# Linear attention on one core: the first loads as row halves on two queues, two more crossbar blocks of 128 rows, and a shorter warming matmul

## The chip, the core and the metric

The kernel runs on one core of one Trainium2 chip. The core has five engines with an instruction stream each: TensorE (PE; its weight loads are shown apart as PEld), VectorE (DVE), ScalarE (ACT), GpSimd (POOL) and SyncE (SP). SP and ScalarE also issue DMA transfers, each on a hardware queue of its own; in the profile SP's queue is q1 and ScalarE's is q10. The metric is the device time of one execution in microseconds. A profile is one more execution, recorded by the hardware profiler; its span runs from the first to the last recorded instruction.

## The reference

x has 2048 rows of 640 columns, wqkv is 640 x 1920, wo is 640 x 640, all bf16. There are 32 heads of 20 columns.

```python
qkv = (x @ wqkv)                       # split into q, k, v, 32 heads of 20
phi = lambda t: where(t > 0, t + 1, exp(t)) + 1e-6
pq, pk = phi(q), phi(k)
kv  = einsum("bhsd,bhse->bhde", pk, v)
z   = einsum("bhsd->bhd", pk)
num = einsum("bhqd,bhde->bhqe", pq, kv)
den = einsum("bhqd,bhd->bhq", pq, z)[..., None] + 1e-6
return merge_heads(num / den) @ wo
```

## The kernel before

Rows are worked in 16 tiles of 128, columns in five blocks of 128. A small planner (`Plan`) holds one list of operations for each engine, in the order in which they are added, and derives the semaphore waits from the tiles that an operation reads and writes. Each engine runs its list in order, so the order of the code is the order of the work. Each DMA has a semaphore of its own and counts as done when all of its bytes have landed.

The stages are these. First k = x Wk for all 16 tiles (`k_half`, L293): TensorE needs x transposed, xT, with the 640 columns of x on the partitions in five blocks, and the five row blocks of Wk, wk0 to wk4. `k_phi` applies phi on ScalarE and VectorE. Then P = xᵀ pk is accumulated over the tiles (`p_step`, L320), which needs x untransposed (`xn`), in turns with the q tiles (`q_tile`, L346). The state, the denominators and the product with wo follow (L433, L457, L475), and the last stage is the output matmuls (L497).

xT comes in two ways. For the first two row tiles (`NPE = 2`) plain DMAs load x into `xn`, TensorE transposes it against an identity (`transpose_x`, L199), and VectorE and ScalarE copy the results from PSUM to xT (L211; ScalarE takes the first two column blocks of tile 1). For rows 256 to 2047, `load_xT` issues DMA transposes (the crossbar) on SP's queue, L185: four blocks of 128 rows (tiles 2 to 5), then five of 256 (two tiles each). `XCH` lists the row ranges. The first of them waits until x tile 0 has landed.

The head of the two DMA queues, `load_wk`, is written out by hand. A word such as "x01" is x tile 0 (from 0, up to 1) and "w23" is Wk block 2:

```python
for eng, what in (("sp", "x01 w01 w23 w45"), ("act", "x12 w12 w34")):
```

So SP issues x tile 0, wk0, wk2 and wk4, ScalarE x tile 1, wk1 and wk3, each one a transfer of 128 rows of 1280 bytes. Behind its four SP has the crossbar blocks, and then `load_rest`: wqn (the weights of q), x tiles 2 to 15 in three transfers, the weights of v, and wo.

While these land, TensorE runs `warm`, matmuls on a constant whose results nobody reads:

```python
warm(512, 512, 512, 512, 512, 512)
order = "t0 t1 k00 k10 k01 k11 k02 k12 k03 k13 k04 k14"
```

"t0" transposes tile 0, and "k10" multiplies tile 1 with wk0, in two halves of 320 output columns. Tiles 0 and 1 are thus worked together, one Wk block after another: two tiles by two halves are four matmuls for each block. From tile 2 on each tile takes its ten matmuls in one go.

Of the kernel before, what the change touches and what calls it, by code (L numbers as in the profile page):

```python
# [82 lines left out]
def bass_standalone__linear_attn_block__prompt_kernel(nc, x, wqkv, wo, out):  # L83
    B, S, D = x.shape
# [10 lines left out]
    with contextlib.ExitStack() as ctx:  # L95
        es = ctx.enter_context

        def sb(name, cols, dt=BF16):
            return es(nc.sbuf_tensor(name, [128, cols], dt))

        xT = sb("xT", NC_ * S)
        xn = sb("xn", NT * D)
        wk = sb("wk", NC_ * D)
# [29 lines left out]
        P = Plan(nc, es)  # L133

        def bank(b, n=BK, off=0, parts=128):
            return ps[0:parts, BK * b + off:BK * b + off + n]
# [9 lines left out]
        def pool_const():  # L146
# [27 lines left out]


        NPE = 2
        XCH = [(128 * t, 128 * t + 128) for t in range(NPE + 4)] + [
            (a, min(a + 256, S)) for a in range(128 * NPE + 512, S, 256)]

        def xch_of(row):  # L180
            return next(i for i, (a, b) in enumerate(XCH) if a <= row < b)

        def load_xT():
            for i, (a, b) in enumerate(XCH[NPE:]):
                P.add("sp", lambda e, a=a, b=b: e.dma_start_transpose(  # L185
                    xT[:, :].rearrange("p (c s) -> p c s", s=S)[:, :, a:b], x[0, a:b, :]),
                    reads=[("xn", 0)] if i == 0 else [],
                    writes=[("xT", NPE + i)], dma=True)

        def transpose_x(st, b_lo, b_hi):  # L190
            groups = ((0, 2, b_lo), (2, NC_, b_hi))

            def columns(b):
                return bank(b, HALF).bitcast(BF16).rearrange("p (c s) -> p c s", s=128)

            def mm(lo, hi, b):
                def go(e):
                    for c in range(lo, hi):
                        r = e.transpose(columns(b)[:, c, :],  # L199
                                        xn[:, st * D + 128 * c:st * D + 128 * c + 128],  # L200
                                        ident[:, :])
                    return r
                P.add("pe", go, reads=xn_keys(st) + ["ident"], writes=[("bank", b)])
            if b_lo == b_hi:
                mm(0, NC_, b_lo)
            else:
                for g in groups:
                    mm(*g)
            for lo, hi, b in groups:
                eng = "act" if st == 1 and lo == 0 else "dve"  # L210
                P.add(eng, lambda e, lo=lo, hi=hi, b=b, eng=eng: (  # L211
                    e.copy if eng == "act" else e.tensor_copy)(
                    xT[:, :].rearrange("p (c s) -> p c s", s=S)[
                        :, lo:hi, 128 * st:128 * st + 128], columns(b)[:, lo:hi, :]),
                    reads=[("bank", b)], writes=[("xT", st, lo)])

        def xT_keys(a, b, cs=range(NC_)):
            keys = []
            for i, (p, q) in enumerate(XCH):
                if p < b and a < q:  # L220
                    keys += [("xT", i)] if i >= NPE else sorted(
                        {("xT", i, 0 if c < 2 else 2) for c in cs})
            return keys
# [7 lines left out]
        def load_xn(a, b, eng):  # L231
            P.add(eng, lambda e: e.dma_start(
                xn[:, a * D:b * D].rearrange("p (t n) -> p t n", n=D),
                x[0, 128 * a:128 * b, :].rearrange("(t p) n -> p t n", p=128)),
                writes=[("xn", t) for t in range(a, b)], dma=True)

        def load_wk():
            tl = mybir.InstLoadActFuncSet(
                name=nc.get_next_instruction_name(),
                act_func_set_id=ACT_TABLE_SET_LN_EXP, ins=[], outs=[])  # L240
            P.add("act", lambda e: e.add_instruction(tl), writes=["table"])
            for eng, what in (("sp", "x01 w01 w23 w45"), ("act", "x12 w12 w34")):
                for k in what.split():
                    a, b = int(k[1]), int(k[2])
                    if k[0] == "x":
                        load_xn(a, b, eng)
                    else:
                        P.add(eng, lambda e, a=a, b=b: e.dma_start(
                            wk[:, a * D:b * D].rearrange("p (c n) -> p c n", n=D),
                            wqkv[128 * a:128 * b, D:2 * D].rearrange("(c p) n -> p c n", p=128)),  # L250
                            writes=[("wk", c) for c in range(a, b)], dma=True)

        def xn_keys(t):
            return [("xn", t)]

        def load_rest():
            w_cols(wqn, 0, D, 0, "wqn", "sp")
            for a, b in ((2, 6), (6, 11), (11, 16)):
                load_xn(a, b, "sp")
            w_cols(wv, 0, D, 2 * D, "wv", "sp")  # L260
            P.add("sp", lambda e: e.dma_start(
                wog[0:GW, 0:5 * D].rearrange("p (g n) -> p g n", n=D),
                wo[0:5 * GW, :].rearrange("(g p) n -> p g n", p=GW)),
                writes=["wog"], dma=True)
            P.add("sp", lambda e: e.dma_start(
                wog[0:gsz[5], 5 * D:6 * D], wo[5 * GW:D, :]), writes=["wog5"], dma=True)
# [12 lines left out]
        def warm(*cols):  # L279
            for n in cols:  # L280
                P.add("pe", lambda e, n=n: e.matmul(
                    bank(4, n), one[:, 0:128], one[:, 0:n], start=True, stop=True),
                    writes=[("bank", 4)])

        def k_banks(st):
            return (2, 0, 4, 6)[st] if st < 4 else 2 + 2 * ((st - 1) % 3)

        def k_half(st, h, cs=range(NC_)):
            b = k_banks(st)

            def mm(e):
                for c in cs:
                    r = e.matmul(  # L293
                        bank(b + h, HALF),
                        xT[:, c * S + 128 * st:c * S + 128 * st + 128],
                        wk[:, c * D + HALF * h:c * D + HALF * (h + 1)],
                        start=(c == 0), stop=(c == NC_ - 1))
                return r
            P.add("pe", mm, reads=xT_keys(128 * st, 128 * st + 128, cs) + [("wk", c) for c in cs],
                  writes=[("bank", b + h)])  # L300

        def k_phi(st):
# [13 lines left out]
        def p_step(h, st, ds=range(NC_)):  # L316

            def mm(e):
                for d in ds:
                    r = e.matmul(  # L320
                        bank(d, HALF), xn[:, st * D + 128 * d:st * D + 128 * d + 128],
                        pk[:, st * D + HALF * h:st * D + HALF * (h + 1)],
                        start=(st == 0), stop=(st == NT - 1))
                return r
            P.add("pe", mm, reads=xn_keys(st) + [("pk", st)],
                  writes=[("bank", d) for d in ds])
# [223 lines left out]

        pool_const()
        load_wk()
        load_xT()
        load_rest()
        warm(512, 512, 512, 512, 512, 512)
        order = "t0 t1 k00 k10 k01 k11 k02 k12 k03 k13 k04 k14"
        for k in order.split():
            st = int(k[1])
            if k[0] == "t":
                transpose_x(st, *((6, 5), (7, 4))[st])  # L560
            else:
                for h in range(2):
                    k_half(st, h, (int(k[2]),))
        for st in range(2):
            k_phi(st)
        for st in range(2, NT):
            k_half(st, 0)
            k_half(st, 1)
            k_phi(st)
            if st in (4, 5):  # L570
                p_step(0, st - 4, range(2))
            if st >= NT - 2:
                permute_wq((0,) if st == NT - 2 else range(1, NC_))
# [139 lines left out]
```

## Time and profile before

| | us |
|---|---|
| median of three timed runs | 99.47 |
| lowest and highest | 99.46, 100.04 |
| the profiled execution | 99.94 |
| its span | 98.7 |

| engine | busy, us | share of the span |
|---|---|---|
| VectorE | 74.7 | 76% |
| ScalarE | 51.0 | 52% |
| GpSimd | 3.5 | 4% |

How to read the profile's rows. The page groups instructions by line, engine and operation. The chain of work that ended last is followed back from the last instruction, from each step to what released it. A row of it gives its start, its length and the engine, line and count. A timeline row has start, length, engine, line, operation, what is written and read, the form, the count, and in brackets the idle time before it with what ended it. A q behind an engine's name marks its sequencer; for a DMA the length is that of the issuing instruction, and the landing comes later. Busy times of matmuls overlap, because they are pipelined: the pace is read from start to start. A row of a stretch gives from and to, the length, busy time and count by engine, the granted TensorE clock (1 is full speed), the busy share of the 16 DMA engines and GB/s. A row on a queue in a stretch gives packets, megabytes and the share of the 16 engines' time. A row of DMA issues ends with the median time from issue to landing.

### The profile page before, as it was taken

How to read it: one execution, taken by the hardware profiler on the slowest of the kernel's cores; microseconds unless marked ns; L12 is line 12 of the kernel's file. 1: busy time of each engine (PE TensorE's matmuls, PEld its weight loads, DVE VectorE, ACT ScalarE, POOL GpSimd, SP SyncE). 2: the span in 40 equal slices, each digit the busy share in tenths (PEclk: the TensorE clock that was granted, in tenths of full speed). 3: DMA queues.
4: the chain of work that ended last, by engine and by line, in shares of the span. 5: the costliest groups of instructions: out<-in, count | busy, mean ns of one | idle time of the engine just before them, and what ended most of it. 6: DMA issues, size and time to landing. Idle time of an engine off the chain costs nothing.

```text
span 98.7 us, 1679 instructions
## 1 busy us (share of the span) xinstructions
PE 95.4 (97%) x656; PEld 62.5 (63%) x662; DVE 74.7 (76%) x139; ACT 51.0 (52%) x84; POOL 3.5 (4%) x15
## 2 busy tenths in 40 slices
PE   6999999999999999999999999999999999999992
PEld 2567777777777666656676556755446776667771
DVE  0214987888889897999959769999979995929332
ACT  5105553455599202472342476289796749665322
POOL 6800000000000000000000000000000000000000
DMA  1995799979999930000000000006410233321534
GB/s 22 362 214 122 153 173 145 219 209 368 375 362 328 207 77 3 0 0 0 0 7 0 0 0 0 0 0 165 115 62 0 92 107 133 133 73 66 199 133 133
DMA packets 17236, 11.73 MB, mean 119 GB/s; under 512 B 9933, under 2 KB 17229, under 8 KB 17229
## 3 DMA queue, kind: packets, MB, share of 16 engines
q1 hardware_dynamic: 16653, 11.10, 42.3%
q10 hardware_dynamic: 576, 0.53, 1.5%
q8 instruction: 5, 0.08, 0.4%
q14 instruction: 2, 0.02, 0.1%
HBM read 5.90 MB, written 2.62 MB: 86 GB/s over the span
## 4 chain that ended last, share of the span: by engine, by line
PE 87%; DVE 6%; DMA 3%; ACT 1%; issue 1%
PE ps L293 23%; PE ps L497 22%; PE ps L346 21%; PE ps L320 17%; DMA xn<-in_x_dram 3%; DVE za L367 3%; PE ps L457 2%; PE ps L433 1%; DVE pq L361 1%; PE ps L199 1%; ACT eq L354 1%; PE ps L475 1%; DVE eq L358 1%; DVE pt L335 0%; PE ps L407 0%
## 5 line engine op out<-in xcount | busy, mean ns | idle before, releaser
L320 PE MATMUL ps<-pk,xn 128*128 128x320 bf16 x160 | 24.0, 299 | 0.0
L346 PE MATMUL ps<-xT,wqp 128*128 128x512 bf16 x95 | 23.1, 379 | 0.3
L293 PE MATMUL ps<-wk,xT 128*128 128x320 bf16 x160 | 23.0, 305 | 0.0
L497 PE MATMUL ps<-w2p,pq 128*128 128x320 bf16 (+3 forms) x170 | 22.3, 291 | 0.1
L354 ACT ACTIVATE eq<-ps 128x512 bf16<-128x512 f32 x20 | 11.9, 597 | 17.1 <-PE ps L346 17.0
L320 PEld LDWEIGHTS ps<-pk,xn 128*128 128x128 bf16 x160 | 15.6, 98 | 7.5
L293 PEld LDWEIGHTS ps<-wk,xT 128*128 128x128 bf16 x160 | 15.9, 100 | 6.5 <-ACT xT L211 0.2
L497 PEld LDWEIGHTS ps<-w2p,pq 128*128 128x128 bf16 x170 | 15.9, 98 | 6.3 <-DVE pq L489 0.2
L306 ACT ACTIVATE ek<-ps 128x640 bf16<-128x640 f32 x16 | 11.2, 704 | 11.8 <-PE ps L293 11.2
L346 PEld LDWEIGHTS ps<-xT,wqp 128*128 128x128 bf16 x100 | 9.7, 98 | 9.2
L361 DVE SCALAR_TENSOR_TENSOR pq<-ps,eq 128x512 bf16<-128x512 f32 x20 | 13.8, 692 | 0.7
L311 DVE SCALAR_TENSOR_TENSOR pk<-ps,ek 128x640 bf16<-128x640 f32 x16 | 13.2, 824 | 0.5
L422 DVE SCALAR_TENSOR_TENSOR ua<-pq,zc,ua 128x512 f32<-128x512 bf16 x12 | 9.0, 748 | 1.1 <-ACT ua L418 0.9
L308 DVE TENSOR_SCALAR ek<-ek 128x640 bf16<-128x640 bf16 x16 | 5.2, 325 | 6.0 <-ACT ek L306 6.0
L489 DVE TENSOR_TENSOR pq<-pq,rd 128x512 bf16<-128x512 bf16 x20 | 7.4, 418 | 2.8 <-ACT rd L482 2.8
L358 DVE TENSOR_SCALAR eq<-eq 128x512 bf16<-128x512 bf16 x20 | 5.8, 289 | 3.4 <-ACT eq L354 3.2
L534 ACT CAST osb<-ps 128x640 bf16<-128x640 f32 x9 | 6.2, 688 | 3.6 <-PE ps L497 3.4
L522 DVE CAST osb<-ps 128x320 bf16<-128x320 f32 (+2 forms) x8 | 3.5, 435 | 3.3 <-PE ps L497 3.1
L367 DVE TENSOR_TENSOR za<-pk 128x1280 f32<-128x1280 bf16 x4 | 5.8, 1483 | 0.0
L519 ACT CAST osb<-ps 128x320 bf16<-128x320 f32 (+1 forms) x8 | 3.1, 404 | 4.7 <-PE ps L497 4.5
L367 DVE TENSOR_TENSOR za<-za 128x1280 f32<-128x1280 f32 x3 | 4.4, 1483 | 0.0
L271 ACT COPY wqp<-wqn 128x640 bf16<-128x640 bf16 x5 | 4.3, 934 | 0.0
(43 smaller groups left out, 45.2 us busy)
## 6 DMA issues: line engine op xcount, KB each, us to landing
out_dram<-osb SPq DMA_DIRECT2D x15, 160.0 KB, 1.8
xn<-in_x_dram SPq DMA_DIRECT2D x2, 800.0 KB, 10.4
wqn<-in_wqkv_dram SPq DMA_DIRECT2D x1, 800.0 KB, 6.6
wv<-in_wqkv_dram SPq DMA_DIRECT2D x1, 800.0 KB, 13.7
wog<-in_wo_dram SPq DMA_DIRECT2D x1, 750.0 KB, 13.5
w2p<-w2g SPq DMA_DIRECT2D x5, 150.0 KB
xn<-in_x_dram SPq DMA_DIRECT2D x1, 640.0 KB, 7.8
wk<-in_wqkv_dram SPq DMA_DIRECT2D x3, 160.0 KB, 4.1
```

The lines of the kernel that those rows point to most:

```text
L293: r = e.matmul(bank(b + h, HALF), xT[:, c * S + 128 * st:c * S + 128 * st + 128], wk[:, c * D + HALF * h:c * D + HALF * (h + 1)], start=(c ...
L306: P.add("act", lambda e: e.activation(fold(t[:, :]), two_banks(b), ACTF.Exp), reads=banks + ["table"], writes=[("ek", st % 3)])
L311: P.add("dve", lambda e: e.scalar_tensor_tensor(fold(pk[:, st * D:(st + 1) * D]), two_banks(b), 0.0, fold(t[:, :]), ALU.max, ALU.add), rea ...
L320: r = e.matmul(bank(d, HALF), xn[:, st * D + 128 * d:st * D + 128 * d + 128], pk[:, st * D + HALF * h:st * D + HALF * (h + 1)], start=(st ...
L346: r = e.matmul(bank(b), wqp[:, d * D + 128 * c:d * D + 128 * c + 128], xT[:, d * S + BK * sbk:d * S + BK * (sbk + 1)], start=(d == 0), sto ...
L354: P.add("act", lambda e: e.activation(t[:, :], bank(b), ACTF.Exp), reads=[("bank", b), "table"], writes=[("eq", i)])
L358: P.add("dve", lambda e: e.tensor_scalar(t[:, :], t[:, :], 1.0, 1e-6, ALU.min, ALU.add), reads=[("eq", i)], writes=[("eq", i)])
L361: P.add("dve", lambda e: e.scalar_tensor_tensor(pq[:, c * S + BK * sbk:c * S + BK * (sbk + 1)], bank(b), 0.0, t[:, :], ALU.max, ALU.add), ...
L367: P.add("dve", lambda e: e.tensor_tensor(d_ap, a, b, ALU.add), reads=ra + rb, writes=[dst])
L422: P.add("dve", lambda e: e.scalar_tensor_tensor(dst[:, :], v, z, a[:, :], ALU.mult, ALU.add), reads=[("pq", s, c), "zc", key], writes=[dkey])
L489: P.add("dve", lambda e: e.tensor_tensor(v, v, rd[i][:, BK * o:BK * (o + 1)], ALU.mult), reads=[("rd", sbk), ("pq", sbk, c)], writes=[("pq ...
L497: r = e.matmul(bank(b, hi - lo), pq[:, c * S + 128 * st:c * S + 128 * st + 128], w2p[:, c * D + lo:c * D + hi], start=(c == 0), stop=(c == ...
```

## The change

The first four transfers of 128 rows (x tiles 0 and 1, wk0 and wk1) become two of 64 rows each. Rows 0 to 63 of each go on SP's queue, and rows 64 to 127 on ScalarE's, in the same order on both: x tile 0, x tile 1, wk0, wk1. The whole blocks wk2, wk3 and wk4 then all go on ScalarE's queue, which issues seven transfers instead of three; SP issues four, as before, now of 64 rows. Whoever reads one of the four split tiles waits for both of its halves; among them is the first crossbar block on SP's queue.

The crossbar blocks become six of 128 rows (tiles 2 to 7) and four of 256. The last of the six warming matmuls has 128 columns in place of 512. Nothing else differs: the order of the operations on TensorE, VectorE and GpSimd is the same, and so is that on ScalarE behind its loads.

```diff
         NPE = 2
-        XCH = [(128 * t, 128 * t + 128) for t in range(NPE + 4)] + [
-            (a, min(a + 256, S)) for a in range(128 * NPE + 512, S, 256)]
+        SPLIT = (0, 1)
+        XCH = [(128 * t, 128 * t + 128) for t in range(NPE + 6)] + [
+            (a, min(a + 256, S)) for a in range(128 * NPE + 768, S, 256)]
...
-                    reads=[("xn", 0)] if i == 0 else [],
+                    reads=xn_keys(0) if i == 0 else [],
...
-            for eng, what in (("sp", "x01 w01 w23 w45"), ("act", "x12 w12 w34")):
+            for eng, what in (("sp", "h00 h10 g00 g10"), ("act", "h01 h11 g01 g11 w23 w34 w45")):
                 for k in what.split():
                     a, b = int(k[1]), int(k[2])
                     if k[0] == "x":
                         load_xn(a, b, eng)
+                    elif k[0] == "h":
+                        P.add(eng, lambda e, a=a, b=b: e.dma_start(
+                            xn[64 * b:64 * b + 64, a * D:(a + 1) * D],
+                            x[0, 128 * a + 64 * b:128 * a + 64 * b + 64, :]),
+                            writes=[("xn", a, b)], dma=True)
+                    elif k[0] == "g":
+                        P.add(eng, lambda e, a=a, b=b: e.dma_start(
+                            wk[64 * b:64 * b + 64, a * D:(a + 1) * D],
+                            wqkv[128 * a + 64 * b:128 * a + 64 * b + 64, D:2 * D]),
+                            writes=[("wk", a, b)], dma=True)
...
         def xn_keys(t):
-            return [("xn", t)]
+            return [("xn", t, 0), ("xn", t, 1)] if t in SPLIT else [("xn", t)]
...
-            P.add("pe", mm, reads=xT_keys(128 * st, 128 * st + 128, cs) + [("wk", c) for c in cs],
+            P.add("pe", mm, reads=xT_keys(128 * st, 128 * st + 128, cs)
+                  + [("wk", c, b) for c in cs if c < 2 for b in range(2)]
+                  + [("wk", c) for c in cs if c > 1],
...
-        warm(512, 512, 512, 512, 512, 512)
+        warm(512, 512, 512, 512, 512, 128)
```

## The prediction

> **What bounds the kernel now.** I read the page first (engines, then the chain that ended last), then the chain in order of time, then the timeline of the first 13 us, since everything that the diff touches lies there. From the page:
>
> ```profile
> PE 95.4 (97%) x656; PEld 62.5 (63%) x662; DVE 74.7 (76%) x139; ACT 51.0 (52%) x84; POOL 3.5 (4%) x15
> ```
>
> The chain in order of time:
>
> ```profile
> 0.80 2.81 DMA xn<-in_x_dram
> 3.61 0.05 issue
> 3.66 1.25 PE ps L199 x10
> 4.91 7.48 PE ps L293 x50
> ...
> 12.65 1.36 PE ps L293 x10
> ...
> 14.28 13.58 PE ps L293 x100
> 27.87 4.89 PE ps L320 x36
> ```
>
> TensorE is the bound, and the only piece of the chain in the first 28 us that isn't TensorE is the landing of x tile 0 at 0.80 + 2.81 = 3.61 us. From 3.66 on TensorE works without a hole. So the change can act in two ways only: by when TensorE starts on tile 0, and by how fast or how interrupted it runs just after. The timeline of the head:
>
> ```profile
> 0.82 0.39 ACTq L232 DMA_DIRECT2D xn<-in_x_dram  x1
> 0.83 2.72 PE L281 MATMUL ps<-const-bfloat16-1.0 128*128 128x512 bf16 x6 [0.83 <-PEq L698]
> ...
> 1.25 1.37 SPq L248 DMA_DIRECT2D wk<-in_wqkv_dram  x3
> 1.25 0.94 ACTq L248 DMA_DIRECT2D wk<-in_wqkv_dram  x2
> ...
> 3.63 12.05 SPq L185 DMA_TRANSPOSE xT<-in_x_dram  x8
> ...
> 4.62 0.37 ACT L211 COPY xT<-ps 128x256 bf16<-128x256 bf16 x1 [2.55 <-PE ps L199]
> ...
> 4.70 7.68 PE L293 MATMUL ps<-wk,xT 128*128 128x320 bf16 x50
> ```
>
> The warming matmuls end at 0.83 + 2.72 = 3.55, just ahead of the tile. TensorE's pace changes inside the 50 matmuls, which the busy time of L293 alone shows:
>
> ```profile
> 4.69:6.02 1.33, 1.32 (x5) 0.72 (x6) 1.00 1.18 298
> ```
>
> Five 320-column matmuls in 1.33 us are 0.266 us each; the chain above has ten of them in 1.36 us at 12.65, 0.136 each. The granted clock column reads 1.00 here all the same, so the step is to be read from the spacing. If n of the 50 ran at 0.266, n x 0.266 + (50 - n) x 0.136 = 7.48 gives n = 5 to 6: the step to full speed lies near 4.70 + 6 x 0.266 = 6.3 at the latest, about 6.1.
>
> **The halves of x.** Before, tile 0 is alone on SP's queue and tile 1 on ScalarE's; landings follow from issue plus time to landing:
>
> ```profile
> xn<-in_x_dram ACTq DMA_DIRECT2D x1, 160.0 KB, 3.0
> wk<-in_wqkv_dram SPq DMA_DIRECT2D x1, 160.0 KB, 3.2
> wk<-in_wqkv_dram ACTq DMA_DIRECT2D x1, 160.0 KB, 3.4
> wk<-in_wqkv_dram SPq DMA_DIRECT2D x1, 160.0 KB, 4.1
> wk<-in_wqkv_dram ACTq DMA_DIRECT2D x1, 160.0 KB, 4.7
> wk<-in_wqkv_dram SPq DMA_DIRECT2D x1, 160.0 KB, 4.5
> ```
>
> That is x0 3.61, x1 3.82, wk0 4.45, wk1 4.65, then wk2 5.8 (issued at 1.25 + 1.37/3), wk3 6.4 (1.25 + 0.47), wk4 6.7. From x1 to wk1 two tiles take 0.83 us: 0.42 per tile, the engines being full. What the two queues had moved early, from 1.8 to 2.5 and from 2.5 to 3.2 us:
>
> ```profile
> q1 hardware_dynamic: 44, 0.06, 64.3%
> q10 hardware_dynamic: 2, 0.00, 1.6%
> ```
> ```profile
> q10 hardware_dynamic: 114, 0.14, 54.7%
> q1 hardware_dynamic: 105, 0.12, 47.7%
> ```
>
> ScalarE's queue (q10) starts late. At 2.5 us, 44 of x0's 128 row packets are through, and the remaining 84 share the engines one to one with x1's: 168 packets, at 219 in 0.7 us some 0.54 us. After the change a queue holds 64 of x0's rows, then 64 of x1's. If ScalarE's lag stays as it is, x0 is complete when its 64 are, together with 64 of SP's: 128 packets, 0.41 us, a gain of 0.13. If both queues start together, all of x0 goes ahead of all of x1 and it lands one tile before the pair is complete: 3.82 - 0.42 = 3.40, a gain of 0.21. Above that, a pair that starts sooner could give up to 0.4; below, the gain is nothing or a small loss if the second issue on each queue (one costs 0.39 to 0.47) holds something up. I take 0.20, nearer to the row of the full engines: x0 at 3.41, transposes at 3.46.
>
> **Shorter warming.** Six matmuls of 512 columns cost 2.72 us with a tail; starts are about 0.43 apart, so the sixth, begun at 2.9, blocks the array to about 3.35. With 128 columns it blocks to about 3.03. Both lie ahead of 3.41, so the cut itself gives nothing and costs nothing on the path, unless x0 lands before 3.35. It leaves an idle stretch of 3.46 - 3.03 = 0.4 us where before there were 3.66 - 3.35 = 0.3.
>
> **What an earlier start is worth.** 0.20 us of earlier work is added at the low pace. If the step to full speed stays at its place (6.1), half of it is kept, 0.10; if it moves along, all 0.20. I take 0.15.
>
> **The rest of the head.** x1 lands with the pair, at 3.8 or a little before; its transposes come after five of x0's ten (1.25/10 each, less overlap about 0.11), at 3.46 + 0.53 = 3.99: 0.2 to spare. The k matmuls need wk0 at 4.70, wk1 at 4.70 + 4 x 0.266 = 5.76, wk2, wk3 and wk4 at about 6.6, 7.1 and 7.7, all 0.2 sooner now. Seven tiles in the same order at 0.42 each give wk0 at about 4.2, wk1 4.65, wk2 5.1, wk3 5.5, wk4 5.9; ScalarE issues them in steps of 0.47 (0.94 for two), its seventh at 0.82 + 6 x 0.47 = 3.6, so that even a landing 3.0 after issue (the row of x1) is 6.6 for wk4, and 4.7 for a wk0 issued at 1.7. This last is the one narrow place: a bound of 0.2 us of wait against 4.5, from a row with a slow start in it; from the packet rates no wait. ScalarE's queue is issuing until 0.82 + 7 x 0.47 = 4.1; behind it stands the copy that ran at 4.62 and would now run at 4.42. Hidden, 0.3 to spare.
>
> **The crossbar blocks.** Issue and landing of the four blocks of 128 rows, then of the five of 256:
>
> ```profile
> L185 SPq DMA_TRANSPOSE xT<-in_x_dram x4: 1262/1282/1313, 3.6 to 7.6; - x4
> ...
> DMA to landing us min/median/max: 3.0/3.5/3.7
> ```
> ```profile
> L185 SPq DMA_TRANSPOSE xT<-in_x_dram x5: 1400/1898/2212, 8.9 to 15.7; - x5
> ...
> DMA to landing us min/median/max: 4.4/4.7/5.4
> ```
>
> The first waits for both halves of x0 and starts at 3.43 instead of 3.63. Behind this wait on SP stand only the other blocks and the later loads. Tiles 6 and 7 landed at 8.9 + 4.5 = 13.4 against a need at 14.28 and now come as two blocks: tile 6 issued at 3.43 + 4 x 1.33 = 8.75, landed by 12.4; tile 7 by 13.8 against 15.4. The first block of 256 (tiles 8 and 9) issues at about 11.4 and lands at 15.8 to 16.8; the need is 14.28 + 2 x 1.36 - 0.2 = 16.8. Covered, barely at the worst. One long issue (1.4 to 2.2) becomes two of 1.3, so all that follows on SP comes 0.4 to 1.2 later, less 0.2:
>
> ```profile
> wqn<-in_wqkv_dram SPq DMA_DIRECT2D x1, 800.0 KB, 6.6
> ...
> xn<-in_x_dram SPq DMA_DIRECT2D x1, 640.0 KB, 7.8
> ```
> ```profile
> 17.97 0.58 SPq L226 DMA_DIRECT2D wqn<-in_wqkv_dram  x1
> 18.61 2.27 SPq L232 DMA_DIRECT2D xn<-in_x_dram  x3
> ```
> ```profile
> 27.15 0.91 ACT L271 COPY wqp<-wqn 128x640 bf16<-128x640 bf16 x1
> ```
>
> wqn landed at 24.6 for a copy at 27.15, x tile 2 at 26.4 for the products that begin at 27.87 (tile 2 after four matmuls, 28.4). At least 1.0 is left of both. No gain, no cost.
>
> **Sum.** -0.15 (bounds -0.4 and +0.1). The profiled execution took 99.94 us with a span of 98.7, 0.47 above the median 99.47 of the three timed runs (99.46 to 100.04). Its own sum is 99.79; on the median it is 99.32, and I forecast 99.3.
>
> **Rivals.** *The halves bring nothing.* The second half is late on ScalarE's queue by as much as the first is early, x0 lands at 3.6, and only the idle stretch grows: 99.45 to 99.5. For it: the rows of q10. Against it: the packet count above still leaves 0.13. The Trainium skill's "DMA: Bandwidth & Descriptors" (Rules for kernel authors) speaks for it too: two transfers to disjoint partition halves share the same 16 engines, so one should not bother. The rows agree that the engines are shared, but here the halves change which tile goes first, not the rate.
>
> *The step to full speed comes late* (slower). This decides if the step needs TensorE to be busy for some stretch with few holes: the hole ahead of tile 0 grows from 0.3 to 0.4 us (0.6 if x0 isn't early), and activity before it may no longer count. Price: the step came 6.1 - 0.83 = 5.3 us after the first warming matmul; if that count starts again at 3.46 it comes at 8.7, and 2.6 us more at half pace lose 1.3, less the gain of 0.15 to 0.2: 100.6. If the step is only put off by the 0.3 us cut from the warming, 99.5. Against it: the hole of 0.3 was tolerated, and 0.1 more is little. By the Trainium skill's "TensorE: Matmul & The Clock Gate" (Part 1) the pace is set by a free-running window of about 3.4 us; missing one would cost an estimated 1.7 us instead, about 101; no row here shows a window.
>
> *The step comes early.* The runs differ by 0.6 us among themselves, and nothing in the middle can absorb that, so its place may vary. If it fell at the first transposes, (6.1 - 3.66)/2 = 1.2 us and the 0.2 would be gained: 98.1; half of that, 98.7.
>
> *A load comes late*: wk0, wk1 or tile 8 by 0.2 to 0.6, 99.5 to 99.9. For it, ScalarE's queue carries five tiles instead of three; against it, the packet rates.
>
> **Chances.** Forecast (99.0 to 99.45) 0.50; halves without effect 0.14; late step 0.20 (0.16 of it above 1%); early step 0.11, most of it over 1% faster; late load 0.05. A difference of 1% (0.99 us) is about what a measurement of this kernel can tell from no change. Faster by that: 0.11; slower: 0.16; within: 0.73. The range leaves out the full late step and the far end of the early one: 98.7 to 100.4.
>
> **What would show it.** The first transpose at 3.4 to 3.5 and x0's landing at 3.4 (right), or at 3.6 (halves without effect). The spacing of L293 falling from 0.266 to 0.136 at about 6.1: at 8 or later the late step is right. No idle time ahead of L293 between 4.5 and 8.2; if there is, a weight block is late. Tile 8's block landed by 16.6. The forecast is wrong if any TensorE idle stretch shows after the first transpose.

## The result and the profile after

The changed kernel takes 103.97 us (median of six executions, 102.39 to 104.43), the kernel before 99.65 (six, 99.37 to 100.04). The ratio is 1.035, with a 95% interval of 1.030 to 1.040. Ratios here and below count only the executions within 1.5% of the fastest of their kernel, medians count all, so the two can differ where executions lie in two groups. The profiled execution took 103.48 us with a span of 102.2; the span is 3.5 us longer than before. The forecast was 99.3.

The page of the changed kernel, its engines and its chain:

```profile
PE 97.7 (96%) x662; PEld 62.3 (61%) x662; DVE 74.7 (73%) x139; ACT 51.1 (50%) x84; POOL 3.5 (3%) x15
...
PE 90%; DMA 5%; ACTq 2%; ACT 1%; DVE 0%; issue 0%
```

The chain in order of time, which before went from the landing of x0 straight to TensorE (its pieces named issue, 0.03 to 0.05 us between these, are left out here):

```profile
0.81 0.61 ACT L242
1.45 0.86 ACTq L249
2.34 0.62 ACTq L254
2.99 0.62 ACTq L254
3.64 5.07 DMA wk<-in_wqkv_dram
8.75 7.15 PE ps L304 x42
```

Two kinds of piece are new: ScalarE's queue issuing one transfer after another until 3.61 us, and a transfer of a Wk block (wk2) that takes 5.07 us. TensorE enters the chain at 8.75 instead of 3.66. The timeline of the head, with the issues and TensorE's pieces:

```profile
0.80 1.24 SPq L249 DMA_DIRECT2D xn<-in_x_dram  x2
...
0.84 1.47 ACTq L249 DMA_DIRECT2D xn<-in_x_dram  x2
...
2.08 1.24 SPq L254 DMA_DIRECT2D wk<-in_wqkv_dram  x2
...
2.34 1.27 ACTq L254 DMA_DIRECT2D wk<-in_wqkv_dram  x2
...
3.44 9.63 SPq L186 DMA_TRANSPOSE xT<-in_x_dram  x7
3.45 0.69 PE L200 MATMUL ps<-ident,xn 128*128 128x128 bf16 x5 [0.21 <-issue]
...
3.64 1.84 ACTq L259 DMA_DIRECT2D wk<-in_wqkv_dram  x3
...
4.51 0.69 PE L200 MATMUL ps<-ident,xn 128*128 128x128 bf16 x5 [0.37 <-DMA xn<-in_x_dram]
...
5.46 1.23 PE L304 MATMUL ps<-wk,xT 128*128 128x320 bf16 x4 [0.26 <-issue]
...
6.99 1.25 PE L304 MATMUL ps<-wk,xT 128*128 128x320 bf16 x4 [0.30 <-DMA wk<-in_wqkv_dram]
```

The first transpose starts at 3.45. Then TensorE stands still four times: ahead of tile 1 (3.45 + 5 x 0.107 = 3.98, next start 4.51), ahead of wk0 (5.04 to 5.46), wk1 (6.53 to 6.99) and wk2 (8.05 to 8.75). That is 0.53 + 0.42 + 0.46 + 0.70 = 2.1 us. One issue of a half takes about 0.62 us (1.24 for two), where a whole tile took 0.39 to 0.47. The second half of x1 on ScalarE's queue took 0.86, and each of the three whole blocks behind the halves 0.53 to 0.64.

The pace of the k matmuls, the stretch 8.75 to 11.42 and the next:

```profile
8.75:11.42 2.67, 2.67 (x11) 1.34 (x12) 1.00 1.19 211
11.42:12.78 1.36, 1.36 (x12) 0.98 (x11) 1.00 0.99 203
```

(The counts include one or two that overlap the edge.) Ten matmuls fill the 2.67 us at 0.267 us each, and from 11.4 on ten take 1.36. So 18 k matmuls ran at half pace, against five or six before: 12 x 0.131 = 1.6 us. The step to full speed came at 11.4 us instead of 6.1. Together: 2.1 of standing, 1.6 of half pace, 0.21 gained at the start; 3.5, as the spans say. Behind tile 1's last k matmul the distance stays the same: the 100 k matmuls that began at 14.28 begin at 17.80, the last 80 matmuls at 90.70 instead of 87.17.

The landings of the later halves of x1, wk0 and wk1, then of wk2 and wk4:

```profile
xn<-in_x_dram ACTq DMA_DIRECT2D x1, 80.0 KB, 2.9
...
wk<-in_wqkv_dram ACTq DMA_DIRECT2D x1, 80.0 KB, 3.0
...
wk<-in_wqkv_dram ACTq DMA_DIRECT2D x1, 80.0 KB, 4.0
```
```profile
wk<-in_wqkv_dram ACTq DMA_DIRECT2D x1, 160.0 KB, 5.1
```
```profile
wk<-in_wqkv_dram ACTq DMA_DIRECT2D x1, 160.0 KB, 5.8
```

x1's later half is there at 1.45 + 2.9 = 4.4 (3.82 before), wk0's at 2.34 + 3.0 = 5.3 (4.45), wk1's at 2.99 + 4.0 = 7.0 (4.65), wk2 at 3.64 + 5.1 = 8.7 (5.8), wk4 at 4.83 + 5.8 = 10.7 (6.7). The rates beside them. First the kernel before, then the changed one:

```profile
2.80:3.60 0.80, 0.75 (x2) 0.00 (x0) 0.00 (x0) 0.00 (x0) 0.80 (x3) 1.00 1.06 387
3.60:4.40 0.80, 0.74 (x8) 0.75 (x9) 0.29 (x1) 0.00 (x0) 0.66 (x4) 1.00 1.03 359
```
```profile
2.80:3.60 0.80, 0.59 (x4) 0.18 (x3) 0.00 (x0) 0.00 (x0) 0.80 (x3) 1.00 0.89 189
3.60:4.40 0.80, 0.54 (x5) 0.28 (x3) 0.51 (x2) 0.00 (x0) 0.66 (x4) 1.00 0.80 192
4.40:5.20 0.80, 0.69 (x5) 0.45 (x5) 0.14 (x1) 0.00 (x0) 0.23 (x1) 1.00 0.80 250
5.20:6.00 0.80, 0.54 (x3) 0.19 (x4) 0.36 (x1) 0.37 (x1) 0.00 (x0) 1.00 1.20 179
```

The last column, GB/s, is about halved in the first two rows, while the DMA share beside it falls only from 1.03 to 1.06 to 0.80 to 0.89: the engines are mostly not idle, but for the same bytes they are held 1.5 to 1.7 times as long.

### The profile page after: what moved, and what is told of

It is laid out like the page before. It is cut to its first block, busy times and chain, and to the rows that moved or that the text cites. A ratio compares the mean times of both kernels' runs of the same rounds, so it can differ in the third digit from the quotient of the medians.

```text
span 102.2 us, 1694 instructions
## 1 busy us (share of the span) xinstructions
PE 97.7 (96%) x662; PEld 62.3 (61%) x662; DVE 74.7 (73%) x139; ACT 51.1 (50%) x84; POOL 3.5 (3%) x15
## 4 chain that ended last, share of the span: by engine, by line
PE 90%; DMA 5%; ACTq 2%; ACT 1%; DVE 0%; issue 0%
PE ps L304 22%; PE ps L510 21%; PE ps L333 21%; PE ps L359 21%; DMA wk<-in_wqkv_dram 5%; PE ps L470 2%; PE ps L446 1%; ACTq L254 1%; PE ps L488 1%; ACTq L249 1%; ACT L242 1%; PE ps L420 0%; DVE osb L535 0%
## 5 line engine op out<-in xcount | busy, mean ns | idle before, releaser
L304 PE MATMUL ps<-wk,xT 128*128 128x320 bf16 x160 | 24.9, 318 | 1.1 <-DMA wk<-in_wqkv_dram 0.8
L359 PE MATMUL ps<-xT,wqp 128*128 128x512 bf16 x100 | 24.2, 379 | 0.0
L319 ACT ACTIVATE ek<-ps 128x640 bf16<-128x640 f32 x16 | 11.2, 704 | 14.4 <-PE ps L304 13.8
```

Source lines behind the costliest of these rows:

```text
L304: r = e.matmul(bank(b + h, HALF), xT[:, c * S + 128 * st:c * S + 128 * st + 128], wk[:, c * D + HALF * h:c * D + HALF * (h + 1)], start=(c ...
L319: P.add("act", lambda e: e.activation(fold(t[:, :]), two_banks(b), ACTF.Exp), reads=banks + ["table"], writes=[("ek", st % 3)])
L359: r = e.matmul(bank(b), wqp[:, d * D + 128 * c:d * D + 128 * c + 128], xT[:, d * S + BK * sbk:d * S + BK * (sbk + 1)], start=(d == 0), sto ...
```

## The experiments

Three questions: which part of the change does the harm, what makes the halves slow, and what makes the later Wk blocks slower still.

**The two small edits alone.**

```diff
-XCH: four blocks of 128 rows, then 256      warm(512, 512, 512, 512, 512, 512)
+XCH: six blocks of 128 rows, then 256       warm(512, 512, 512, 512, 512, 128)
```

> The kernel before with only the two small edits: six crossbar blocks of 128 rows and the last warming matmul of 128 columns. Theory H (halves): the harm comes from the transfers of 64 rows, whose issue takes 0.6 us against 0.43 for 128 rows, so that the first four tiles arrive at half the rate; then this kernel stays within 0.3 us of before (99.4 to 99.9). Theory Q (queue): the harm comes from wk2 to wk4 standing last on ScalarE's queue and moving beside the crossbar's packets; the same, 99.4 to 99.9. Theory W (warming): the shorter warming puts off the step of TensorE to full speed; 100.2 to 101 and the step in the spacing of the k matmuls at 7 us or later instead of 6.1.

Ratio 1.003 (1.000 to 1.005), median 99.94 against 99.78. TensorE in the head:

```profile
4.73 7.10 PE L293 MATMUL ps<-wk,xT 128*128 128x320 bf16 x50
```

The first 1.36 us of these fifty hold nine, where the kernel before has six in its first 1.36 us: the step came by 4.7 here, ahead of the first k matmul and earlier than in the kernel before. Theory W falls.

**The queue alone**, whole tiles:

```diff
-("sp", "x01 w01 w23 w45"), ("act", "x12 w12 w34")
+("sp", "x01 w01"), ("act", "x12 w12 w23 w34 w45")
```

> The kernel before with whole tiles, but wk2 and wk4 on ScalarE's queue: SP issues x0 and wk0, ScalarE x1, wk1, wk2, wk3, wk4. Theory H: no 64-row transfers, so wk4 is issued by 3.2 us, is there by 6.7, and the time is that of before, 99.4 to 99.9. Theory Q: the weights on the other queue share the engines with the crossbar blocks, wk3 and wk4 land at 7.5 us or later, TensorE waits for them, 100.5 to 102.

Ratio 0.998 (0.996 to 1.001). ScalarE issued its last block at 2.7 and wk4 landed at 6.6, as H said. Moving the blocks is harmless by itself.

**The halves alone**, wk2 and wk4 on SP's queue as before:

```diff
-("sp", "x01 w01 w23 w45"), ("act", "x12 w12 w34")
+("sp", "h00 h10 g00 g10 w23 w45"), ("act", "h01 h11 g01 g11 w34")
```

> x0, x1, wk0 and wk1 as row halves on both queues, but wk2 and wk4 behind them on SP's queue (ahead of the crossbar) and wk3 on ScalarE's; warming and crossbar blocks as before. Theory H: x1 lands at about 4.3, wk0 at 5.3 and wk1 at 6.3 as in the changed kernel, wk2 to wk4 follow within 1.5 us; TensorE waits 1.5 to 2 us and the step to full speed comes late; 101.5 to 103.5. Theory Q: with the weights ahead of the crossbar the waits for wk1 and wk2 go, which are more than half of the loss; 99.8 to 101.

Ratio 1.016 (1.011 to 1.021), median 101.22, just under H's range. x1 landed at 4.7, wk0 at 5.1, wk1 at 7.0 and wk4 at 8.1. So the halves alone cost 1.6%, the queue alone nothing, and both together 3.5%: the rest arises only where the halves make the blocks late and wk2 to wk4 all stand behind them on ScalarE's queue.

**Only x in halves**, Wk whole:

```diff
-("sp", "x01 w01 w23 w45"), ("act", "x12 w12 w34")
+("sp", "h00 h10 w01 w23 w45"), ("act", "h01 h11 w12 w34")
```

> Only x0 and x1 as row halves on both queues; the five blocks of Wk whole and on the queues of before, warming and crossbar blocks as before. Theory H: x0 at 3.4, x1 at 4.3, wk0 at about 5.0, the rest soon after, for two issues more of 0.6 us a queue: a wait of 0.5 us for x1 and 0.4 for wk0, 100.2 to 101.5. Theory Q: nothing is moved behind the crossbar's start, 99.3 to 99.9.

Ratio 1.007 (1.004 to 1.010), from five executions of 100.1 to 100.5, at the lower end of H and above Q. Five more took 101.7 to 102.2, the profiled one among them, so its trace doesn't explain the ratio.

**Which rows, which shape.** Is it that a half reaches only 64 neighbouring partitions? Every second row instead:

```diff
-xn[64 * b:64 * b + 64, ...], x[0, 128 * a + 64 * b:128 * a + 64 * b + 64, :]
+xn[b:128:2, ...],            x[0, 128 * a + b:128 * a + 128:2, :]      (Wk alike)
```

> The changed kernel with one thing different: each half holds every second row (even rows on SP's queue, odd rows on ScalarE's) and so goes to every second partition of all 128, not to the upper or lower 64. The same 64 rows per transfer, the same queues and order. Theory P (partitions): the transfer to 64 neighbouring partitions moves at half rate because it reaches only half of the memory's inlets; then x1 lands by 3.9, wk0 by 4.4, wk1 by 5.0, the DMA engines move over 330 GB/s between 2.8 and 4.8 us, and the time is 99.5 to 100.8. Theory H (issue): a transfer of 64 rows takes 0.6 us to issue whatever the rows are; the landings stay at 4.4, 5.4 and 6.9 and the time at 103 to 104.5.

Median 103.9 (102.08 to 105.03). The rates after 2.8 and 3.6 us stay low, and the halves issue as slowly (0.56 to 0.75 us each):

```profile
2.80:3.60 0.80, 0.60 (x4) 0.16 (x3) 0.00 (x0) 0.00 (x0) 0.80 (x3) 1.00 0.88 202
3.60:4.40 0.80, 0.56 (x5) 0.29 (x3) 0.50 (x2) 0.00 (x0) 0.66 (x4) 1.00 0.84 263
```

Theory P falls: which partitions a half reaches is not the cause. Next, halves by columns, 128 rows of 640 bytes:

```diff
-xn[64 * b:64 * b + 64, a * D:(a + 1) * D]
+xn[:, a * D + 320 * b:a * D + 320 * (b + 1)]      (Wk alike)
```

> The changed kernel with its halves cut by columns: 128 rows of 640 bytes on each queue, same tiles, queues and order. Theory P: all 128 partitions are reached, x1 by 3.9, wk0 by 4.4, 99.3 to 100.5. Theory H: 128 rows to a transfer are issued in 0.43 us, with the same result, 99.3 to 100.5. A theory S (small transfers of any shape are slow, each having its own wait): landings as in the changed kernel, 102.5 to 104.5.

Ratio 1.021 (1.016 to 1.025): below the changed kernel, above all that H and P gave. The issue was quick, as H said:

```profile
0.80 0.87 SPq L249 DMA_DIRECT2D xn<-in_x_dram  x2
0.84 0.87 ACTq L249 DMA_DIRECT2D xn<-in_x_dram  x2
```

x1 landed at 3.7, ahead of the 3.82 of the kernel before. But wk0 landed at 5.2 and wk4 at 9.5. So a quick issue is not enough, and H alone falls too. Theory S isn't met either: the time is below its range, and x1 came 0.7 us earlier than in the changed kernel, but wk0 hardly earlier (5.2 against 5.3).

**One tile in halves, both on one queue**, to measure the issue:

```diff
-("sp", "x01 w01 w23 w45"), ("act", "x12 w12 w34")
+("sp", "h00 h01 w01 w23 w45"), ("act", "x12 w12 w34")
```

> Only x tile 0 as row halves, both on SP's queue; all else whole, ScalarE's queue as before. Measures the issue by itself: if a transfer of 64 rows costs 0.6 us of issue whoever issues beside it, SP's two take 0.6 each and ScalarE's whole ones 0.39 to 0.46. If 0.6 comes of both queues issuing halves at once, SP's take 0.4. Time 99.5 to 100.8, since wk0 is issued 0.8 us later.

```profile
0.80 1.23 SPq L249 DMA_DIRECT2D xn<-in_x_dram  x2
0.84 0.38 ACTq L233 DMA_DIRECT2D xn<-in_x_dram  x1
```

SP's two halves take 0.6 us each while ScalarE's whole tile beside them takes 0.38. The cost belongs to the transfer of 64 rows, not to the crowd. The time was 102.95 (two executions), far above the 99.5 to 100.8 expected: the second half, issued at 1.46, landed only at 5.4, and TensorE began 1.8 us late. The rates at that time:

```profile
3.20:3.60 0.40, 0.36 (x1) 0.00 (x0) 0.00 (x0) 0.00 (x0) 0.40 (x1) 1.00 0.82 122
3.60:4.00 0.40, 0.00 (x0) 0.00 (x0) 0.00 (x0) 0.00 (x0) 0.33 (x3) 1.00 0.70 99
```

By 2.2 us five transfers of 640 KB in all had been issued, and until 3.2 about 380 KB had been moved. So the rate fell to 99 GB/s with issued work outstanding.

**Only x0 in halves, one on each queue.**

> Only x tile 0 as row halves, one on each queue; behind them whole tiles: SP x1, wk1, wk3, ScalarE wk0, wk2, wk4. Theory H: x0 at 3.35, x1 issued at 1.45 (half an issue late) and landed at 4.1 to 4.4, wk0 at 4.5 to 4.8; a hole of 0.2 to 0.5 us at x1 and the gain of 0.2 at x0 about cancel, 99.3 to 100.2.

Inconclusive: four executions, 100.11, 100.19, 102.1 and 102.5, no interval. In the profiled one (100.11) x0's later half landed at 3.8, x1 at 4.7 and wk0 at 5.2, all later than H said.

**x0 and x1 in columns, Wk whole:**

> x0 and x1 as column halves (128 rows of 640 bytes) on both queues; the Wk blocks whole and where they were; warming short, crossbar as before. From the landings of the run with column halves: x0 3.25, x1 3.7; wk0 is third on its queue and is issued at 1.72. If whole blocks keep the full rate, wk0 lands at 4.3 to 4.5 as TensorE needs it at 4.4, and the time is 0.1 to 0.4 us below before. If it lands at 4.8 or later, the gain is lost: equal or up to 0.5 us slower.

Inconclusive too: one execution at 99.53, five at 101.4 to 102.3. In the profiled one (102.22) wk0, issued at 1.72, landed at 5.6; that is late, as the second case feared, and the loss is larger than the 0.5 us it allowed. No gain showed in either run.

**Do the engines run dry?** A new theory was needed: halves carry few bytes per issue, so the stock of issued work is used up, and behind that point each packet shows its own delay. First, x0 alone in columns, with whole tiles right behind:

```diff
-("sp", "x01 w01 w23 w45"), ("act", "x12 w12 w34")
+("sp", "h00 x12 w12 w34"), ("act", "h01 w01 w23 w45")     (h by columns; short warming)
```

> Only x tile 0 as column halves, one on each queue (issued in 0.4 us each); behind them whole tiles: SP x1, wk1, wk3, ScalarE wk0, wk2, wk4. Theory R (the engines run dry): a head that supplies fewer bytes per issue than the engines move leaves them idle, and from then on each packet shows its own delay. Here the second issue on each queue already carries a whole tile, the stock never runs out, the engines hold 330 to 390 GB/s from 2.8 to 4.4 us, x1 and wk0 land at 4.1 to 4.4 and the time is 99.0 to 99.9. Theory X (a cut tile spoils the transfers behind it): wk0 lands at 5 us or later as in the run with x0 and x1 in columns, 101 to 102.3.

Ratio 1.003 (1.000 to 1.006), median 99.99.

```profile
2.80:3.60 0.80, 0.78 (x6) 0.38 (x5) 0.00 (x0) 0.00 (x0) 0.80 (x3) 1.00 0.84 250
3.60:4.40 0.80, 0.44 (x6) 0.18 (x4) 0.65 (x2) 0.00 (x0) 0.66 (x4) 1.00 0.95 319
4.40:5.20 0.80, 0.80 (x7) 0.61 (x7) 0.15 (x1) 0.37 (x1) 0.23 (x1) 1.00 1.06 383
```

The rate dips behind the two halves and recovers once whole tiles are queued; x1 landed at 4.3 and wk0 at 4.6. X falls. R is nearer but not met: it had 330 to 390 GB/s from 2.8 to 4.4, and the rows show 250 and 319. Second, a gap in the supply with no half in it, wk0 and wk1 held back until 2.74:

> The kernel before with whole tiles throughout, but wk0 and wk1 are issued only when the fourth warming matmul has ended (about 2.75 us instead of 1.25), so that the engines have moved x0 and x1 and run out of work by 3.4. Theory R: the blocks behind the gap move at 200 to 300 GB/s between 3.6 and 5.2 instead of 360, wk0 lands 2.6 to 3.0 us after its issue (5.3 to 5.7), and later blocks fall beside the crossbar and land at 7 to 9; 101 to 102.5. Theory X: with no cut tile the rate behind the gap is the full 360 to 390, wk0 lands at 5.0 to 5.2 and wk4 by 7.2; 100 to 100.8.

```profile
3.60:4.40 0.80, 0.79 (x8) 0.80 (x9) 0.33 (x2) 0.00 (x0) 0.66 (x4) 1.00 0.66 61
4.40:5.20 0.80, 0.46 (x5) 0.19 (x2) 0.62 (x2) 0.37 (x1) 0.24 (x1) 1.00 0.92 328
5.20:6.00 0.80, 0.28 (x3) 0.21 (x3) 0.05 (x1) 0.00 (x0) 0.00 (x0) 1.00 1.09 395
```

Ratio 1.007 (1.004 to 1.010). Between 3.6 and 4.4 the DMA share is 0.66 at 61 GB/s: a few packets hold their engines for long, with whole tiles only. wk0 landed at 5.7, R's figure. But the full rate is back by 5.2, and wk4 landed at 7.3, nearer to X's; the time too is X's. So a gap costs the block behind it, not all that follow. That eight small transfers in a row keep the stock low in the changed kernel would fit, but no run shows it, and e8 above speaks against it: its rate fell while issued work was outstanding.

**Beside the crossbar.** The changed kernel with the first crossbar block held until wk4 has landed:

> The changed kernel with the first crossbar block held until wk4 has landed, so that no weights and crossbar packets move at the same time. Theory B (beside): the weights on ScalarE's queue are slow from 5 us on because the engines switch between them and the crossbar's packets; then wk2, wk3 and wk4 land by 7.5 instead of 8.7, 9.7 and 10.7, and TensorE waits later instead, for tile 2's block (3.5 us after wk4). Theory I (issue): they are late because ScalarE issues them at 3.6, 4.3 and 4.8; then they land at 8 to 10 as before. The time is 102 to 105 in both, since the wait for tile 2 takes the place of the others.

wk2 and wk4:

```profile
wk<-in_wqkv_dram ACTq DMA_DIRECT2D x1, 160.0 KB, 3.2
```
```profile
wk<-in_wqkv_dram ACTq DMA_DIRECT2D x1, 160.0 KB, 2.9
```

Issued at 3.64 and 4.79 as before the hold, they land at 6.8 and 7.7 instead of 8.7 and 10.7: B's side, by 1.9 and 3.0 us. Median 103.88 (two executions), since the crossbar's blocks then came late, as both expected; the chain waits for tile 3's until 12.69. The other way round, whole tiles with wk2 to wk4 held until x0 has landed:

> The kernel before with whole tiles; wk2, wk3 and wk4 on ScalarE's queue, held back until x tile 0 has landed, so that they are issued from 3.6 to 5 us as in the changed kernel, beside the first crossbar blocks. No transfer of 64 rows in it. Theory B (beside the crossbar): being beside the crossbar is what makes them late; wk2 lands at 7.5 to 8.7, wk4 at 9.5 to 10.7, and the time is 101.5 to 103.5. Theory H alone (halves): late issue costs only its own delay, 3 us from issue to landing as in the head; wk2 6.5, wk3 7.0, wk4 7.5, and 99.6 to 100.3.

wk2 and wk3, issued at 3.69 and 4.06:

```profile
wk<-in_wqkv_dram ACTq DMA_DIRECT2D x1, 160.0 KB, 2.6
```
```profile
wk<-in_wqkv_dram ACTq DMA_DIRECT2D x1, 160.0 KB, 4.2
```

wk2 lands at 6.3, ahead of most of the crossbar's packets, wk3 at 8.3 and wk4 at 8.7. Ratio 1.011 (1.008 to 1.014), median 100.56: more than H alone allows, less than B named. So late loads beside the crossbar slip without any half, if less than in the changed kernel. This run also has a gap in the supply ahead of wk2, but wk2 itself, the block right behind the gap, took only 2.6 us.

**The holes filled**, six constant matmuls put ahead of tile 1, wk0, wk1 and wk2:

> The changed kernel with six matmuls of 512 columns on a constant put into TensorE's holes (ahead of tile 1's transposes, of the first k matmul, and two each ahead of wk1 and wk2). They do no work of the reference. Theory C (clock): the step to full speed came at 11.4 us because of the holes; with TensorE busy it comes between 4.5 and 8, the k matmuls after wk2 run at 0.136 us, and the time falls by 1 to 1.6 us, to 102 to 103. Theory D (delay alone): the step does not hang on the holes, 103.5 to 104.5.

Ratio 1.038 (1.033 to 1.043), median 103.47: no gain, the lower edge of D. Yet the step came earlier, at about 8.8, if not as early as C said (4.5 to 8):

```profile
7.78 1.19 PE L304 MATMUL ps<-wk,xT 128*128 128x320 bf16 x4
8.80 0.60 PE L571 MATMUL ps<-const-bfloat16-1.0 128*128 128x512 bf16 x2
9.24 1.25 PE L304 MATMUL ps<-wk,xT 128*128 128x320 bf16 x8
11.25 1.94 PE L304 MATMUL ps<-wk,xT 128*128 128x320 bf16 x13 [0.77 <-DMA wk<-in_wqkv_dram]
```

Eight in 1.25 us from 9.24 on are at full pace; then TensorE waits for wk4, landed at 11.2. In the profiled execution of the changed kernel wk4 landed at 10.7, so at full pace its four matmuls would have started there and tile 2 at about 11.25; it started at about 11.7. Of the 1.6 us of half pace only some 0.4 was therefore not covered by the wait for wk4.

No variant beat the kernel before; the best, the queue alone, equals it.

## Why the prediction was wrong

Right were the first steps: x0 landing at 0.84 + 2.5 = 3.34 (3.41 forecast), the first transpose at 3.45 (3.46), the start 0.21 earlier (0.20), and that the two small edits, with the crossbar's later loads, cost nothing clear of the noise (e1). The gain at x0 shows in more than one profile: TensorE began tile 0 at 3.39 to 3.62 in the six with this head (after, e3, e4, e6, e9, e10) and at 3.61 to 3.84 in five with x0 whole (before, e1, e2, e11, e15). But the reason that I gave, one tile of 0.42 ahead of the pair, isn't what happened: x1 came 1.0 us behind x0. That the figure came out is partly luck.

Wrong was the part "The rest of the head", in two places. The first is "x1 lands with the pair" and "Seven tiles in the same order at 0.42 each". I took the engines' full rate as given and checked only whether the issue kept up, with the issue cost of a whole tile (0.39 to 0.47) put in for a half. A half costs 0.6 (measured alone in e8). So the later halves of x1, wk0 and wk1 were issued 0.63, 1.1 and 1.7 us later than the whole tiles before, and they landed 0.55, 0.9 and 2.3 us later: 1.0 to 1.65 us apart, not 0.42. All of this lateness at x1 and wk0, and most of it at wk1, is later issue. The terms that I called 0 are worth the 1.6% of e3. I had named the issue as a lower bound for wk0 ("a bound of 0.2 us of wait") and didn't follow it down the queue, where each block adds the same delay again. With 3.0 us from issue to landing, the prediction's own figure, and the issue times as measured, wk0 comes out at 5.3, as it did. Issue alone is not the whole cause: in e7, whose halves were issued in 0.4 to 0.45, wk0 was issued 0.5 us later than before and landed 0.8 later, and the engines moved 181 to 227 GB/s between 3.2 and 4.8.

The second is that the crossbar was priced by SP's queue alone. ScalarE's issuing ended at 5.5, not 4.1, so wk2 to wk4 went out when crossbar packets were already moving; e9 takes 1.9 to 3.0 us off their landings by removing that, and e11 shows a smaller effect with no half. The prediction had a late load as a rival at 0.05, priced at 0.6 us at most; it was the outcome, and was worth six times that. In the profile before, the warning stood in rows that I quoted: by 0.42 a tile from wk1's 4.65 on, wk2, wk3 and wk4 would have landed at 5.1, 5.5 and 5.9 there too, the very figures of the prediction, but they landed at 5.8, 6.4 and 6.7.

The rival of the late step (0.20) was right in its direction and place (11.4; I had said 8 or later), but not in its cause as I gave it: the hole ahead of tile 0 is harmless in e1. The four holes behind it are the likelier cause, since the step came at 8.8 with them filled (e10), but its place also moved between e1 and the kernel before, so one profile doesn't show it. Its price was largely hidden behind wk4.

The rule of the Trainium skill's "DMA: Bandwidth & Descriptors" (Rules for kernel authors) not to bother with two transfers to disjoint partition halves gave the right advice. Its reason, that both halves share the same engines, would by itself mean no gain, not a loss of 1.6% (e3); e6 and e8 show that the issue cost is in the 64 rows of a transfer, not in which partitions they reach.

What stays open: why 64 rows cost more to issue than 128, why halves by columns (e7) land later still than their later issue accounts for, and what holds a packet behind a gap. That the engines run dry fits e15 in part, and e8 doesn't fit it.

## What to carry to other kernels

Before cutting a load to get it sooner, compare bytes per issue over the issue time, for all queues, with the rate that the engines hold: eight halves at 0.62 us supply 2 x 80 KB in that time, 264 GB/s, against the 390 seen before. If it is lower, the first piece comes earlier and everything behind it later; if it isn't, that alone is no proof, as e7 shows. Measure the issue of the new shape; don't take it from the old one. And when loads slip, look at what they slip into: here blocks that landed about 1 us later than before with the DMA transposes held back (e9) landed 3 to 4 us later beside them.

## What the runs showed of the hardware

- A DMA of 64 rows of 1280 bytes took 0.56 to 0.62 us to issue, in single cases 0.70 to 0.86 (the changed kernel, e3, e4, e6); one of 128 rows of 1280 or 640 bytes with no half ahead of it on its queue took 0.34 to 0.46. A half was no quicker when it reached every second partition (e6) or when the other queue issued whole tiles (e8). The first whole tile behind halves on a queue took 0.59 as well in e8, and the two behind that 0.43 each; in the changed kernel all three took 0.53 to 0.64.
- Less warming and a longer hole ahead of tile 0 did not put off the step to full speed: it came at about 6.1 before and by 4.7 in e1. The granted clock column shows 1.00 throughout. In e9 TensorE was busy without a hole from 5.42 and still ran at half pace until 10.45, 0.267 us for a matmul of 320 columns:

```profile
5.42:10.45 5.03, 5.03 (x20) 2.71 (x20) 1.00 0.45 117
```

By the Trainium skill's "TensorE: Matmul & The Clock Gate" (Part 1) the gate looks at free-running windows of about 3.4 us; a window from 7.0 to 10.45 would fit e9. No run here shows the windows themselves.
